# Attention, a routed expert layer and a dense layer on one core: the first job's preparation moved to step ends, masks added per bank, later routing tables made in later jobs

## The chip, the core and the metric

The kernel runs on one core of a Trainium2 chip. The metric is the device time of one execution in microseconds; lower is better. Times inside an execution are counted from the start of its span, the time from the first to the last instruction that the profiler recorded.

The engines are TensorE (PE in the profile, PEld for its weight loads), VectorE (DVE), ScalarE (ACT) and GpSimd (POOL); SyncE (SP) issues most of the transfers. Each engine works through its own instructions in order and waits at a semaphore for what it needs from another one.

## The reference

```python
scores = np.matmul(q, k.transpose(0, 1, 3, 2)) / np.sqrt(64)   # batch 4, 8 heads, 576 positions
rel = pos[:, None] - pos[None, :]
mask_local = (rel >= 0) & (rel < 32)
mask_strided = (rel >= 0) & (pos[None, :] % 32 == pos[:, None] % 32)
scores = where(mask_local if h < 4 else mask_strided, scores, -1e9)
x = softmax(scores) @ v                                        # -> 2304 tokens x 512
logits = x @ w_gate + modality_bias[modality_id]               # 8 experts
e = argmax(logits); gate = softmax(logits)[e]
y[t] = gate[t] * (relu(x[t] @ w1[e]) @ w2[e])                  # 512 -> 1024 -> 512
out = elu(y @ w_in) @ w_out                                    # 512 -> 2048 -> 512
```

All of it is float32. The large products are made of three passes on rounded parts: a value is split into a high part and the rest, which costs ScalarE a copy and VectorE a subtraction.

## The kernel before

**Attention** (line 838 on) takes 32 steps, numbered n from 0: four batches, in each the head pairs 2, 3 (strided mask), 0, 1 (local mask), and two halves of a pair. A step issues, in this order: the scores of step n (`emit_S`, line 983) with their masks and maxima on VectorE and the subtraction of the maxima on GpSimd (line 1010); transposes of q and k for the next pair; transposes of the probabilities of step n-2 (`emit_PT`); the logits of a finished batch, where there is one; transposes of x of step n-5 (`emit_X`); the product with v of step n-3 (`emit_PV`); the exponential of step n-1 on ScalarE; and loads of later steps on SP. A strided unit has eight 72x72 score tiles, four in each of two PSUM banks. One VectorE instruction per tile adds the mask and takes the maximum, and a short readout behind each brings the maximum out (line 1009).

**Routing.** A token goes to the expert of its largest logit. Five jobs of 512 rows are fixed in the program, and a loop at the end takes any that are left (none for these inputs). Job 0 is chosen early, from the first nine blocks of 128 tokens, which exist after step 21: `Router.early` (line 275) ranks the tokens, picks the fullest expert (`star`), makes onehot matrices and a product A on GpSimd (lines 373 and 388), and nine matmuls give the table of row numbers and gates (`finish`, line 390). The rows are gathered by indirect DMAs that GpSimd issues (line 448), scaled by the gates (line 452), transposed by TensorE and split (`trans`, line 459). Weights come by `fetch_to` (SP, two transfers of 256 KB each) and are split by `split_to` (ScalarE and VectorE). This early work is a generator, `early` (line 592). `bg()` runs it on to its next yield; the calls stand in `emit_X` and `emit_PV`, seven or eight in a step. A yield of STEP holds it until `bg.step()`, which each step calls once, behind its product with v.

**Jobs.** A job has eight chunks; a chunk's first product (`gemm1`, lines 485 to 487) and its second (`gemm2`, lines 504 to 506, two chunks later) are cut in four pieces each, a piece being three passes for one of four tiles, and `stream` yields behind each piece. `plan` (line 682) puts other work at piece numbers: the end of attention up to piece 8; logits and choice for the other tokens at 10; ranks of all tokens at 14 (`place`; `rank`, lines 259 and 261, are its matmuls); onehots and A for jobs 1 to 4 at 16 (`first_tables`); the table's matmuls, job 1's number and its gathers at 28; two further tables, for the loop's rows, begun at 30 and 36 and finished at 36 and 44; job 1's scales at 38 and its transposes at 42, 46 and 52; the table of dense places at 53 and 64. The work for jobs 2 to 4 stands inside `stream`. VectorE's copy of a finished table (line 395) and the two or three instructions behind it give the row numbers.

All instructions stand on their engines in the order in which the program issues them.

Of the kernel before, what the change touches and what calls it, by code (L numbers as in the profile page):

```python
# [14 lines left out]
ALU = mybir.AluOpType  # L15
# [14 lines left out]
NT = T // 128  # L30
# [43 lines left out]
class Background:  # L74
# [19 lines left out]

    def step(self):
        self.held = False

    def finish(self):
        while self.gens:
# [69 lines left out]
class Router:  # L169
# [102 lines left out]
        V.tensor_copy(self.lof[:, q, 0:n], self.lo[:, q, 0:n])  # L272
        yield

    def early(self, pool, chosen):

        V = self.tc.nc.vector
        t = lambda shape, dt, name: pool.tile(shape, dt, name=name)
        rank = self.rank(NE, 1)
        yield  # L280
        key = t([128, E], F32, "key")
        kmax = t([128, 1], F32, "kmax")
        z = t([128, NE, E], F32, "z")
        pr = t([128, NE, E], F32, "pr")
        no = t([128, NE], F32, "no")
        sh = [128, NE, E]
        pos = self.pos[:, 0, 0:NE]
        oh = self.oh[:, 0:NE, 1:C]
        V.scalar_tensor_tensor(key, rank[:, NE], 16.0, self.rev, ALU.mult, ALU.add)
        yield  # L290
        V.reduce_max(kmax, key, axis=AX.X)
        yield
        V.tensor_scalar(key, key, kmax, None, ALU.is_equal)
        yield
        V.tensor_tensor(z, oh, key.unsqueeze(1).to_broadcast(sh), ALU.mult)
        yield

        V.scalar_tensor_tensor(pr, rank[:, 0:NE], -4096.0, z, ALU.add, ALU.mult)
        yield
        V.reduce_sum(pos, pr, axis=AX.X)  # L300
        V.tensor_tensor(key[0:1], key[0:1], self.rev[0:1], ALU.mult)
        yield
        V.tensor_scalar(pos, pos, 4096.0, None, ALU.add)
        V.reduce_max(kmax[0:1], key[0:1], axis=AX.X)
        yield
        V.tensor_scalar(self.star, kmax[0:1], -1.0, float(E), ALU.mult, ALU.add)
        chosen()
        yield from self.split_places(0, NE)
        onehot = self.new_onehot(pool)
        yield from self.onehot(0, NE, onehot, self.tc.nc.gpsimd)  # L310
        finish = self.table(pool, onehot, 0, NE, 0, 4, 5, self.idx, self.gates, self.tc.nc.gpsimd)
        yield Background.STEP
        V.tensor_scalar(no, pos, 512.0, None, ALU.is_ge)
        V.tensor_scalar(self.oh[:, 0:NE, 0], pos, 512.0, None, ALU.is_lt)
        yield
        V.tensor_tensor(oh, oh, no.unsqueeze(2).to_broadcast(sh), ALU.mult)
        yield
        finish()
        yield

    def place(self, pool):

# [81 lines left out]
def ffn(tc, ctx, x_dram, part_dram, ident, router, conv, bank, w1, w2, out, run_attention):  # L404
# [46 lines left out]
    def scale(job, c, eng=nc.vector):  # L451
        eng.tensor_scalar(job.xg[c], job.xg[c], job.gate[:, c:c + 1], None, ALU.mult)
# [66 lines left out]
    def new_job(s):  # L519
        word = router.tab[0:1, s, 0:1] if s else router.star  # L520
        e = nc.sync.value_load(word, min_val=0, max_val=E - 1)
        jobs.append(Job(e, None, idx[:, 4 * s:4 * s + 4], gate[:, 4 * s:4 * s + 4]))
# [33 lines left out]
    def fetch_to(g):  # L556
        while loaded[0] <= g:
            s, f = divmod(loaded[0], NCH)
            if s < NS:
                if s == len(jobs):  # L560
                    new_job(s)
                raws[loaded[0]] = fetch(jobs[s], f)
            else:
                fetch2(loaded[0] - NG)
            loaded[0] += 1

    def split_to(g):
        while splits[0] <= g:
            if splits[0] < NG:
                split_w(splits[0] % NW, raws.pop(splits[0]))  # L570
            else:
                split2(splits[0] - NG)
            splits[0] += 1
# [18 lines left out]
    def early():  # L592
        STEP = Background.STEP
        yield from router.choose(0, NE)
        yield from router.early(r_p, lambda: fetch_to(2))
        for c in range(4):
            gather(jobs[0], c)
            yield STEP if c % 2 else None
        for i in range(SPLIT):
            split_to(i)  # L600
            fetch_to(i + AHEAD - SPLIT)
            yield STEP
        for c in range(4):
            scale(jobs[0], c)
            yield STEP if c == 3 else None
        for kk in range(4):
            trans(jobs[0], kk)
            yield STEP if kk % 2 else None

    bg.early = early  # L610
    at = run_attention(bg)
# [4 lines left out]
    def close_b():  # L616
        at.close_b()
        wp = ctx.enter_context(tc.tile_pool(name="w3", bufs=1))
        add_weights(wp, NW - len(WH))
        XT.extend(x_pairs(wp, 2))  # L620
        conv.start(ctx)

    def first_tables():
        oh[0] = router.new_onehot(r_p)
        run(router.onehot(0, NT, oh[0]))
        fin.append(router.table(r_p, oh[0], 0, NT, 4, 20, 5, idx, gate))
        router.blocks(r_p)

    def more_tables(c0):
        fin.append(router.table(r_p, oh[0], 0, NT, c0, c0 + 16, 5, idx, gate))  # L630

    def dense():
        oh[0] = router.new_onehot(r_p)
        run(router.onehot(1, NT, oh[0]))
        fin.append(router.table(r_p, oh[0], 1, NT, 0, NT, 2, idxd, None))

    def open_y():
        rctx.close()
# [2 lines left out]
    def run(gen):  # L641
        for _ in gen:
            pass

    oh, fin = {}, []
    table = lambda: fin.pop()()

    def stream():
# [35 lines left out]
        (3, lambda: at.PV(30)), (3, lambda: at.X(29)), (3, lambda: at.PT(31)),  # L684
        (4, lambda: at.PV(31)), (4, lambda: at.X(30)),
        (5, lambda: at.L(3, 0)), (5, lambda: at.X(31)), (8, lambda: at.L(3, 1)),
        (10, lambda: at.lg(NE, NT)), (10, lambda: run(router.choose(NE, NT))), (10, close_b),
        (14, lambda: run(router.place(r_p))), (16, first_tables),
        (28, table), (28, lambda: new_job(1)), (30, lambda: more_tables(20)), (36, table), (36, lambda: more_tables(36)), (44, table),
        (53, dense), (64, table), (66, open_y),  # L690
    ]
    plan += [(28, lambda c=c: gather(jobs[1], c)) for c in range(4)]
    plan += [(38, lambda c=c: scale(jobs[1], c)) for c in range(4)]
    plan += [(n, lambda kk=kk: trans(jobs[1], kk)) for kk, n in enumerate((42, 46, 52, 52))]
# [18 lines left out]

    lctx = ExitStack()
    x_loop, h_loop = bank("T", "x_ps"), bank("S", "h_ps")
    ahead = [bank("ST"[j], "h2_ps") for j in range(2)]
# [119 lines left out]
def attention(tc, bg, q, k, v, mod, mbias, wg, x_dram, ident, router, bank):  # L838
# [148 lines left out]
    def emit_S(n):  # L987
        b, pr, s = steps[n]
        pi = n // 2
        m, w, nj = shape(pr)  # L990
        pss = [bank("S", f"ps_sc{r}", m, nj, w) for r in range(2)]
        for j in range(nj):
            for r in range(2):

                ro = slice(D * r, D * r + D)
                if pr >= 2:
                    c = (4 * (j % 2) + 2 * s + j // 2) * M
                    ck = c + 32
                else:
                    c = ck = (nj * s + j) * m  # L1000
                nc.tensor.matmul(pss[r][:, j], lhsT=qt[pi % 2][ro, c:c + m],
                                 rhs=kt[pi % 2][ro, ck:ck + w], start=True, stop=True)
        sm = s_p.tile([m, 2 * nj, w], F32, tag="sm", name="sm")
        mx = m_p.tile([m, 2 * nj], F32, tag="mx", name="mx")
        for r in range(2):
            for j in range(nj):
                mk = mask_s if pr >= 2 else (mask_0 if s == 0 and j == 0 else mask_l)
                i = nj * r + j
                nc.vector.tensor_tensor_reduce(sm[:, i], pss[r][:, j], mk, 1.0, -3.0e38, ALU.add, ALU.max, mx[:, i:i + 1])
        nc.gpsimd.tensor_tensor(sm, sm, mx.unsqueeze(2).to_broadcast([m, 2 * nj, w]), ALU.subtract)  # L1010
        st[n] = sm

# [110 lines left out]
    for n in range(NU):  # L1123
        emit_S(n)
        if n + 2 < NU:
            emit_T(n // 2 + 1, 2 * (n % 2))
        if n >= LP:
            emit_PT(n - LP)
        if n + 2 < NU:
            emit_T(n // 2 + 1, 2 * (n % 2) + 1)  # L1130
        if n > LX:
            b, pr, s = steps[n - LX - 1]
            if pr == 1:
                emit_L(b, s)
        if n >= LX:
            emit_X(n - LX)
        if n >= LV:
            emit_PV(n - LV)
        if n == 16 + LX:
            emit_lg(0, NE)  # L1140
            bg.add(bg.early())
        bg.step()
        if n:
            emit_exp(n - 1)
        if n == 5:
            emit_bias()
        if n % 2 == 1:
            p = n // 2 + 3
            if p < 4 * B:
                load_pair(p // 4, PAIRS[p % 4])  # L1150
        if n % 8 == 7 and n + 8 < NU:
            load_vs(n // 8 + 1)
        if n > 8 and n % 8 == 3:
            load_vl(n // 8)
    emit_exp(NU - 1)
    return SimpleNamespace(PT=emit_PT, PV=emit_PV, X=emit_X, L=emit_L, lg=emit_lg, close_a=actx.close, close_b=bctx.close)

# [27 lines left out]
```

## Time and profile before

| | |
|---|---|
| median of 3 runs | 794.57 us (793.63 to 795.36) |
| profiled execution, device time | 794.71 us |
| its span | 793.0 us |
| TensorE busy, share of the span | 763.6 us, 96% |
| VectorE busy | 508.3 us, 64% |
| ScalarE busy | 395.6 us, 50% |
| GpSimd busy | 108.5 us, 14% |
| mean granted clock of TensorE | 0.991 |

Busy time is the union of an engine's instructions. A matmul's end is modelled, so a busy TensorE need not be at its peak. The granted clock is a share of full speed; 0.5 is the lower of two levels. Attention lasts up to about 144 us, the jobs up to about 387 us, the dense layer from there on.

### The profile page before, as it was taken

How to read it: one execution, taken by the hardware profiler on the slowest of the kernel's cores; microseconds unless marked ns; L12 is line 12 of the kernel's file. 1: busy time of each engine (PE TensorE's matmuls, PEld its weight loads, DVE VectorE, ACT ScalarE, POOL GpSimd, SP SyncE). 2: the span in 40 equal slices, each digit the busy share in tenths (PEclk: the TensorE clock that was granted, in tenths of full speed). 3: DMA queues.
4: the chain of work that ended last, by engine and by line, in shares of the span. 5: the costliest groups of instructions: out<-in, count | busy, mean ns of one | idle time of the engine just before them, and what ended most of it. 6: DMA issues, size and time to landing. Idle time of an engine off the chain costs nothing.

```text
span 793.0 us, 12672 instructions
## 1 busy us (share of the span) xinstructions
PE 763.6 (96%) x4513; PEld 636.5 (80%) x4513; DVE 508.3 (64%) x1321; ACT 395.6 (50%) x759; POOL 108.5 (14%) x140
## 2 busy tenths in 40 slices
PE   6999988989999999999899999999999999999995
PEld 5989876868888888888788788888888888888885
DVE  3768779798867677576477565565666454544443
ACT  3667646433544454445376555554565444444442
POOL 4533372022001020000000101001001010101011
PEclk9999999999999999999999999999999999999999
DMA  9587695545566575454232221033133030201111
GB/s 159 120 186 172 151 241 102 153 148 186 179 204 222 172 227 183 163 184 136 93 122 80 94 79 54 27 107 119 41 95 131 1 107 0 84 24 41 66 41 67
DMA packets 100302, 94.37 MB, mean 119 GB/s; under 512 B 45433, under 2 KB 78731, under 8 KB 100235
## 3 DMA queue, kind: packets, MB, share of 16 engines
q1 hardware_dynamic: 95056, 78.79, 34.8%
q0 software_dynamic: 4480, 14.68, 5.4%
q8 instruction: 37, 0.61, 0.3%
q14 instruction: 30, 0.25, 0.1%
q10 hardware_dynamic: 699, 0.04, 0.1%
HBM read 70.95 MB, written 22.54 MB: 118 GB/s over the span
## 4 chain that ended last, share of the span: by engine, by line
PE 50%; POOLq 0%; POOL 0%; DVE 0%; issue 0%
PE o_ps L797 8%; PE o_ps L799 8%; PE o_ps L798 8%; PE h_ps L711 8%; PE h_ps L710 8%; PE h_ps L712 8%; POOLq L1181 0%; POOL out_dram L813 0%; DVE part L812 0%
## 5 line engine op out<-in xcount | busy, mean ns | idle before, releaser
L773 DVE SCALAR_TENSOR_TENSOR t<-e,t 128x512 f32<-128x512 f32 (+1 forms) x80 | 51.1, 638 | 110.7 <-ACT e L771 110.7
L710 PE MATMUL h_ps<-xh,wh 128*128 128x512 f32 (+1 forms) x320 | 119.1, 372 | 2.2 <-PEq L723 2.2
L712 PE MATMUL h_ps<-xh,wl 128*128 128x512 f32 (+1 forms) x320 | 119.3, 373 | 0.0
L711 PE MATMUL h_ps<-xl,wh 128*128 128x512 f32 (+1 forms) x320 | 119.2, 372 | 0.0
L797 PE MATMUL o_ps<-wh,gh 128*128 128x512 f32 x288 | 113.3, 393 | 0.0
L798 PE MATMUL o_ps<-wl,gh 128*128 128x512 f32 x288 | 112.9, 392 | 0.0
L799 PE MATMUL o_ps<-wh,gl 128*128 128x512 f32 x288 | 112.9, 392 | 0.0
L770 ACT ACTIVATE t<-h_ps 128x512 f32<-128x512 f32 (+1 forms) x80 | 44.2, 552 | 99.8 <-PE h_ps L712 92.3
L775 ACT CAST gh<-r 128x512 fp32r<-128x512 f32 (+1 forms) x80 | 46.2, 578 | 81.5 <-DVE r L774 81.5
L776 DVE TENSOR_TENSOR gl<-r,gh 128x512 fp32r<-128x512 f32 (+1 forms) x80 | 51.1, 639 | 51.5 <-ACT gh L775 51.5
L469 DVE TENSOR_TENSOR wl<-wraw,wh 128x1024 fp32r<-128x1024 f32 x56 | 69.2, 1235 | 12.8 <-ACT wh L468 11.0
L710 PEld LDWEIGHTS h_ps<-xh,wh 128*128 128x128 f32 x320 | 60.6, 189 | 14.3 <-issue 2.6
L711 PEld LDWEIGHTS h_ps<-xl,wh 128*128 128x128 f32 x320 | 60.6, 189 | 11.9
L712 PEld LDWEIGHTS h_ps<-xh,wl 128*128 128x128 f32 x320 | 60.5, 189 | 11.0
L504 PE MATMUL y_ps<-hh,wh 128*128 128x512 f32 x160 | 64.6, 404 | 0.0
L797 PEld LDWEIGHTS o_ps<-wh,gh 128*128 128x128 f32 x288 | 54.1, 188 | 12.5 <-DVE o L808 0.7
L799 PEld LDWEIGHTS o_ps<-wh,gl 128*128 128x128 f32 x288 | 54.1, 188 | 12.1
L485 PE MATMUL h_ps<-xh,wh 128*128 128x512 f32 x160 | 63.7, 398 | 0.0
L506 PE MATMUL y_ps<-hh,wl 128*128 128x512 f32 x160 | 63.3, 395 | 0.0
L505 PE MATMUL y_ps<-hl,wh 128*128 128x512 f32 x160 | 63.2, 395 | 0.0
L798 PEld LDWEIGHTS o_ps<-wl,gh 128*128 128x128 f32 x288 | 54.1, 188 | 11.1
L487 PE MATMUL h_ps<-xh,wl 128*128 128x512 f32 x160 | 62.9, 393 | 0.0
(180 smaller groups left out, 1393.4 us busy)
## 6 DMA issues: line engine op xcount, KB each, us to landing
wraw<-in_moe_w_dram SPq DMA_DIRECT2D x80, 256.0 KB
raw<-in_moe_w_in_dram SPq DMA_DIRECT2D x16, 512.0 KB
raw<-in_moe_w_out_dram SPq DMA_DIRECT2D x16, 512.0 KB
w_f<-cv_r SPq DMA_DIRECT2D x32, 256.0 KB
wraw<-w_f SPq DMA_DIRECT2D x16, 512.0 KB
part_dram<-o POOLq DMA_DIRECT2D x18, 256.0 KB, 3.0
part<-part_dram SPq DMA_DIRECT2D x18, 256.0 KB
qn<-in_q_dram SPq DMA_DIRECT2D x8, 288.0 KB
```

What stands on the lines that cost most here:

```text
L469: nc.vector.tensor_tensor(WL[i], raw, WH[i].bitcast(F32), ALU.subtract)
L485: nc.tensor.matmul(ps, lhsT=a, rhs=job.xh[kk], start=kk == 0, stop=False)
L487: nc.tensor.matmul(ps, lhsT=b, rhs=job.xh[kk], start=False, stop=kk == 3)
L504: nc.tensor.matmul(ps, lhsT=a, rhs=hh, start=f == 0, stop=False)
L505: nc.tensor.matmul(ps, lhsT=a, rhs=hl, start=False, stop=False)
L506: nc.tensor.matmul(ps, lhsT=b, rhs=hh, start=False, stop=f == NCH - 1)
L710: nc.tensor.matmul(ps[:, 0:n], lhsT=a, rhs=yh, start=kk == 0, stop=False)
L711: nc.tensor.matmul(ps[:, 0:n], lhsT=a, rhs=yl, start=False, stop=False)
L712: nc.tensor.matmul(ps[:, 0:n], lhsT=b, rhs=yh, start=False, stop=kk == 3)
L797: nc.tensor.matmul(ps, lhsT=a, rhs=WH[i][:, 512:1024], start=first, stop=False)
L798: nc.tensor.matmul(ps, lhsT=a, rhs=WL[i][:, 512:1024], start=False, stop=False)
L799: nc.tensor.matmul(ps, lhsT=b, rhs=WH[i][:, 512:1024], start=False, stop=last)
```

## The change

Six things are done.

1. `flush` empties the background work up to its next STEP, at the end of each attention step. The STEPs in `Router.early` and `early` stand at other places, and the fetches of job 0's weights are begun one by one, not three together.
2. Job 0's scales are made by GpSimd, not by VectorE.
3. For strided units VectorE adds the mask to a whole bank (72x288) in one instruction, twice, and takes all eight maxima with one reduction over 72x576.
4. The three instructions that mark the tokens which job 0 took leave the early work and stand behind the choice for the other tokens, at piece 10 (`others`).
5. The two further tables are begun at pieces 84 and 104 and finished at 100 and 116.
6. The dense places are made three blocks at a time, every fourth piece from 120 on, and finished at 164. Onehots and products have a pool of their own, `late`, closed before the loop.

```diff
 class Background:
+    def flush(self):
+        while self.gens and not self.held:
+            self()
...
-    def early(self, pool, chosen):
+    def early(self, pool, chosen, more):
...
         V.scalar_tensor_tensor(pr, rank[:, 0:NE], -4096.0, z, ALU.add, ALU.mult)
-        yield
+        yield Background.STEP
...
         chosen()
         yield from self.split_places(0, NE)
+        yield Background.STEP
         onehot = self.new_onehot(pool)
-        yield from self.onehot(0, NE, onehot, self.tc.nc.gpsimd)
+        for i, _ in enumerate(self.onehot(0, NE, onehot, self.tc.nc.gpsimd)):
+            yield Background.STEP if i == 1 else None
         finish = self.table(pool, onehot, 0, NE, 0, 4, 5, self.idx, self.gates, self.tc.nc.gpsimd)
+        more()
         yield Background.STEP
-        V.tensor_scalar(no, pos, 512.0, None, ALU.is_ge)
-        V.tensor_scalar(self.oh[:, 0:NE, 0], pos, 512.0, None, ALU.is_lt)
-        yield
-        V.tensor_tensor(oh, oh, no.unsqueeze(2).to_broadcast(sh), ALU.mult)
-        yield
         finish()
         yield
+
+        def others():
+            V.tensor_scalar(no, pos, 512.0, None, ALU.is_ge)
+            V.tensor_scalar(self.oh[:, 0:NE, 0], pos, 512.0, None, ALU.is_lt)
+            V.tensor_tensor(oh, oh, no.unsqueeze(2).to_broadcast(sh), ALU.mult)
+
+        self.others = others
...
     def early():
         STEP = Background.STEP
         yield from router.choose(0, NE)
-        yield from router.early(r_p, lambda: fetch_to(2))
+        yield STEP
+        yield from router.early(r_p, lambda: fetch_to(0), lambda: fetch_to(1))
         for c in range(4):
             gather(jobs[0], c)
-            yield STEP if c % 2 else None
-        for i in range(SPLIT):
-            split_to(i)
-            fetch_to(i + AHEAD - SPLIT)
-            yield STEP
+            yield STEP if c == 1 else None
+        split_to(0)
+        fetch_to(2)
+        yield STEP
+        split_to(1)
+        fetch_to(3)
+        yield
         for c in range(4):
-            scale(jobs[0], c)
-            yield STEP if c == 3 else None
+            scale(jobs[0], c, nc.gpsimd)
+            yield STEP if c == 1 else None
         for kk in range(4):
             trans(jobs[0], kk)
-            yield STEP if kk % 2 else None
+            yield STEP if kk % 2 == 0 else None
...
-    def dense():
-        oh[0] = router.new_onehot(r_p)
-        run(router.onehot(1, NT, oh[0]))
-        fin.append(router.table(r_p, oh[0], 1, NT, 0, NT, 2, idxd, None))
+    def dense(i):
+        if i == 0:
+            oh[0] = router.new_onehot(late[0])
+            oh[1] = router.onehot(1, NT, oh[0])
+        next(oh[1], None)
+        if i == NT // 3:
+            fin.append(router.table(late[0], oh[0], 1, NT, 0, NT, 2, idxd, None))
...
-        (10, lambda: at.lg(NE, NT)), (10, lambda: run(router.choose(NE, NT))), (10, close_b),
+        (10, lambda: at.lg(NE, NT)), (10, lambda: run(router.choose(NE, NT))), (10, lambda: router.others()), (10, close_b),
         (14, lambda: run(router.place(r_p))), (16, first_tables),
-        (28, table), (28, lambda: new_job(1)), (30, lambda: more_tables(20)), (36, table), (36, lambda: more_tables(36)), (44, table),
-        (53, dense), (64, table), (66, open_y),
+        (28, table), (28, lambda: new_job(1)), (66, open_y),
+        (84, lambda: more_tables(20)), (100, table), (104, lambda: more_tables(36)), (116, table), (164, table),
     ]
+    plan += [(120 + 4 * i, lambda i=i: dense(i)) for i in range(NT // 3 + 1)]
...
         for r in range(2):
+            if pr >= 2:
+                nc.vector.tensor_tensor(sm[:, nj * r:nj * r + nj], pss[r], mask_s.unsqueeze(1).to_broadcast([m, nj, w]), ALU.add)
+                continue
             for j in range(nj):
-                mk = mask_s if pr >= 2 else (mask_0 if s == 0 and j == 0 else mask_l)
+                mk = mask_0 if s == 0 and j == 0 else mask_l
                 i = nj * r + j
                 nc.vector.tensor_tensor_reduce(sm[:, i], pss[r][:, j], mk, 1.0, -3.0e38, ALU.add, ALU.max, mx[:, i:i + 1])
+        if pr >= 2:
+            nc.vector.reduce_max(mx, sm, axis=AX.X)
         nc.gpsimd.tensor_tensor(sm, sm, mx.unsqueeze(2).to_broadcast([m, 2 * nj, w]), ALU.subtract)
...
         if n > 8 and n % 8 == 3:
             load_vl(n // 8)
+        bg.flush()
```

## Rows read from the trace of the kernel before

**Rows 1.** The page's first part: busy us (share of the span) and instructions.

```profile
PE 763.6 (96%) x4513; PEld 636.5 (80%) x4513; DVE 508.3 (64%) x1321; ACT 395.6 (50%) x759; POOL 108.5 (14%) x140
```

**Rows 2.** Busy time by stretch; behind the engines granted clock, DMA share, GB/s.

```profile
60.00:80.00 20.00, 20.00 (x294) 18.86 (x291) 17.70 (x125) 14.36 (x38) 7.52 (x6) 1.00 0.73 174
...
92.00:94.00 2.00, 1.08 (x13) 0.94 (x14) 1.97 (x13) 1.45 (x4) 0.10 (x1) 1.00 0.00 0
108.00:114.00 6.00, 5.58 (x68) 5.41 (x69) 5.00 (x29) 3.20 (x7) 4.83 (x5) 0.72 1.01 286
...
124.00:136.00 12.00, 8.61 (x82) 6.66 (x79) 11.75 (x46) 6.57 (x13) 3.79 (x3) 1.00 0.27 66
...
174.00:180.00 6.00, 5.65 (x33) 4.74 (x34) 5.24 (x11) 0.00 (x0) 3.01 (x3) 0.72 0.98 335
```

**Rows 3.** TensorE in order of time, attention: scores of steps 24, 29, 30, table, q.

```profile
95.78 0.74 PE L1001 MATMUL ps_sc<-kt,qt 64*72 64x72 f32 x16
...
108.42 0.37 PE L393 MATMUL tab_ps<-A,onehot 128*128 128x20 bf16 x9 [1.91 <-POOL A L388]
...
115.65 0.44 PE L976 MATMUL ps_tr<-ident,qn 96*128 96x96 f32 x3 [1.32 <-DMA qn<-in_q_dram]
...
119.10 0.90 PE L1001 MATMUL ps_sc<-kt,qt 64*96 64x128 f32 x12
...
123.41 0.90 PE L1001 MATMUL ps_sc<-kt,qt 64*96 64x128 f32 x12
```

**Rows 4.** ScalarE in order of time: the exponential of the logits.

```profile
92.22 0.26 ACT L239 ACTIVATE lg_ex<-lg_d 128x72 f32<-128x72 f32 x1 [1.20 <-DVE lg_d L234]
```

**Rows 5.** VectorE in order of time: step 24's first masked maximum, last readout; marking product.

```profile
98.08 0.21 DVE L1009 CUSTOM_DVE_ANT_0 sm<-ps_sc,mask_s 72x72 f32<-72x72 f32 x1
...
99.30 0.07 DVE L1009 DVE_READ_ACCUMULATOR2_ANT mx<- 72x1 f32 x1
...
106.87 2.71 DVE L316 TENSOR_TENSOR oh<-oh,no 128x72 bf16<-128x72 bf16 x1
```

**Rows 6.** Groups of VectorE by line, 60 to 260 us: count, busy us, mean ns.

```profile
L1066 DVE TENSOR_TENSOR xs<-ps_v,rs 72x256 f32<-72x256 f32 x20 | 7.6, 415 | 0.3
...
L340 DVE TENSOR_REDUCE pos<-places 128x36 f32<-128x324 f32 x1 | 0.5, 491 | 0.0
```

**Rows 7.** GpSimd in order of time: subtractions, onehots, A, gathers of job 1.

```profile
99.54 1.15 POOL L1010 TENSOR_TENSOR sm<-sm,mx 72x576 f32<-72x576 f32 x1 [2.62 <-ACT sm L1014]
101.55 5.26 POOL L373 TENSOR_SCALAR onehot<-iota,pos_lof 128x128 bf16<-128x128 bf16 x9 [0.86 <-DVE rs L1061]
...
107.87 0.50 POOL L388 TENSOR_TENSOR A<-oa,vals 128x180 bf16<-128x180 bf16 x1
...
123.40 1.47 POOL L1010 TENSOR_TENSOR sm<-sm,mx 96x768 f32<-96x768 f32 x1 [5.64 <-DVE mx L1009]
...
171.52 1.57 POOL L448 DMA_INDIRECT xg<-x_dram,idx  x1 [14.89 <-DMA wraw<-in_moe_w_dram]
...
176.67 0.95 POOL L448 DMA_INDIRECT xg<-x_dram,idx  x1 [0.30 <-issue]
```

**Rows 8.** TensorE in order of time, first job: ranks, two tables, job 1's transposes.

```profile
154.19 0.25 PE L259 MATMUL rank<-oh,triu 128*128 128x171 bf16 x1
...
164.98 0.82 PE L393 MATMUL tab_ps<-A,onehot 128*128 128x80 bf16 x18
...
174.35 1.16 PE L393 MATMUL tab_ps<-A,onehot 128*128 128x80 bf16 x18 [2.90 <-DVE A L388]
...
180.81 0.72 PE L463 MATMUL x_ps<-ident,xg 128*128 128x128 f32 x4
```

**Rows 9.** VectorE in order of time, first job: the first table's copy, job 1's scales.

```profile
170.34 0.23 DVE L395 COPY tab_sb<-tab_ps 128x80 f32<-128x80 f32 x1
...
179.42 1.72 DVE L452 TENSOR_SCALAR xg<-xg,gates 128x512 f32<-128x512 f32 x4
```

**Rows 10.** The tile xg, 80 to 270 us: the 16 gathers, from issue to landing.

```profile
DMA to landing us min/median/max: 4.0/5.2/7.6
```

More of the change, by code (lines that the diff above doesn't have):

```diff
@@ L621, in close_b @@
         conv.start(ctx)
+        late.append(tctx.enter_context(tc.tile_pool(name="late", bufs=1)))
     def first_tables():
-        oh[0] = router.new_onehot(r_p)
+        oh[0] = router.new_onehot(late[0])
         run(router.onehot(0, NT, oh[0]))
-        fin.append(router.table(r_p, oh[0], 0, NT, 4, 20, 5, idx, gate))
+        fin.append(router.table(late[0], oh[0], 0, NT, 4, 20, 5, idx, gate))
         router.blocks(r_p)
     def more_tables(c0):
-        fin.append(router.table(r_p, oh[0], 0, NT, c0, c0 + 16, 5, idx, gate))
-    def dense():
-        oh[0] = router.new_onehot(r_p)
-        run(router.onehot(1, NT, oh[0]))
-        fin.append(router.table(r_p, oh[0], 1, NT, 0, NT, 2, idxd, None))
+        fin.append(router.table(late[0], oh[0], 0, NT, c0, c0 + 16, 5, idx, gate))
+    def dense(i):
+        if i == 0:
+            oh[0] = router.new_onehot(late[0])
+            oh[1] = router.onehot(1, NT, oh[0])
+        next(oh[1], None)
+        if i == NT // 3:
+            fin.append(router.table(late[0], oh[0], 1, NT, 0, NT, 2, idxd, None))
     def open_y():
@@ L643, in run @@
             pass
-    oh, fin = {}, []
+    oh, fin, late = {}, [], []
+    tctx = ExitStack()
     table = lambda: fin.pop()()
@@ L712, in up_mm @@
             nc.tensor.matmul(ps[:, 0:n], lhsT=b, rhs=yh, start=False, stop=kk == 3)
+    tctx.close()
     lctx = ExitStack()
```

## The prediction

> **What bounds the kernel now.** The page's first part comes first: TensorE is busy for 763.6 of 793.0 us [rows 1], so at most about 29 us are idle, and only idle time and slow clock are there to be won. The busy time by stretch says where: from 60 to 80 us TensorE is full with VectorE at 17.70 of 20 us; in 92 to 94 it lacks 0.92 us, in 124 to 136 it lacks 12.00 - 8.61 = 3.39 us with VectorE at 11.75 [rows 2]. Then TensorE's own timeline: it waits 1.91 us for GpSimd's product A before the first job's table, 1.32 us for a load of q [rows 3], and 2.90 us for VectorE's A before the second table [rows 8]. The granted clock is at 0.72 in the 6 us after each of the two longest of these waits [rows 2]: the engine, just idle, drops to the lower of its two levels (1.2 instead of 2.4 GHz) for a while, at a loss of 0.28 x 6 = 1.7 us each. The stretch 124 to 136, with shorter waits among its matmuls, stays at 1.00. So the change bears on some 1.9 + 1.3 + 0.9 + 3.4 + 2.9 + 2 x 1.7 = 13.8 us, the most it could win.
>
> **How the pieces move.** The routing work waits in chunks that end at a STEP. The hold is lifted after a step's transposes and value products, and the new flush then empties one chunk at the end of each step. So chunks go out whole, behind each engine's work of that step: the choice of experts after step 21, ranks after 22, places and the first weight fetch after 23, six onehots after 24, three onehots with A after 25, the table with two gathers after 26, two gathers and the first split after 27, the second split and scales 0 and 1 after 28, scales 2 and 3 and the first transposes after 29, the rest after 30 and 31.
>
> **Masks.** Eight masked maxima start at 98.08 and the last readout ends at 99.37: 1.29 us of VectorE [rows 5]. Two additions of 72x288 cost about 0.415 x 288/256 = 0.47 each, a maximum over 576 columns 0.491 x 576/324 = 0.87, from the nearest rows [rows 6], so 1.8 us; with overlap such as the eight show, 1.5. That is 0.2 to 0.5 us more for each of 16 units, not less. I take nothing on the path: TensorE is full there while VectorE has a tenth free [rows 2]. Without this cover, in steps 24 to 27, four units would give 0.8 to 2 us; the bank freed after one addition gives some of it back.
>
> VectorE's groups add up to far more, since each of the eight takes 0.21 and a readout 0.07, 2.3 us a unit; but they start 0.15 apart. The Trainium skill (VectorE: DVE Perf Modes, Rules for kernel authors) says to minimise the number of instructions, because chaining them saves nothing. By that rule the edit would free 0.8 us a unit; by the row it frees none. That is the third rival below.
>
> **Choice of experts.** ScalarE's exponential of the logits waits 1.20 us for VectorE, and the scores' exponential is queued behind it [rows 4]; that is the 0.92 us in 92 to 94. It now stands one step earlier, behind the exponential that was late. Take -0.9 (bounds 0 and -0.9).
>
> **Weights of the first job.** Three fetches of 2 x 256 KB left together ahead of the last pair's q and k. Now one leaves after step 23, behind the loads of that step; the second is queued behind the last pair. SP's load of the expert number still waits for VectorE, with only the next store of x behind it. The wait for q goes: -1.3 (0 to -1.3).
>
> **First table.** On GpSimd the subtraction of step 24 starts 99.54 - 95.78 = 3.8 us after that step's scores; 1.15 + 5.26 + 1.15 + 0.50 = 8.1 us must pass before A exists, cut in two or not [rows 3, 7]. So A comes 11.9 us after the scores. TensorE needs three steps, 108.42 - 1.91 - 95.78 = 10.7 us, or 10.1 if small waits go [rows 3]. It waits 1.2 to 1.8: I take 1.7 in place of 1.91, -0.2 (bounds -0.8, +0.5), and the slow stretch behind it stays.
>
> **Scales on GpSimd, transposes one step sooner.** No row shows this scale. GpSimd's onehots take 5.26/9 = 0.58 us for 128 columns; the subtractions 1.15 for 576 and 1.47 for 768 give 1.67 ns a column, 1.05 us at 512 [rows 7]. Lower bound 0.6 (as a onehot, whatever the width), upper 2.3 (four onehots); I take 1.2, the subtraction's line plus what a onehot lies above it. Scales 2 and 3 are queued behind the subtraction of step 29, which began at 123.40, 4.3 us after that step's scores at 119.10 [rows 3, 7]. So they end at 4.3 + 1.47 + 2.4 = 8.2 us. TensorE is through with step 29 after 123.41 - 119.10 = 4.3 us and stands before a transpose that needs all four rows: 3.9 us; with VectorE 1 us earlier, 2.9. I take 3.4 (2.2 at 0.6 us a scale, 5.6 at 2.3). This is a new wait, and everything of steps 30 and 31 is behind it on TensorE; a third slow stretch, +1.7, follows as behind the wait of 1.91. In return it lets the other engines catch up: of the 3.39 us, 0.4 are left, -3.0 (0 to -3.4).
>
> Attention: -0.9 - 1.3 - 0.2 + 3.4 + 1.7 - 3.0 = -0.3 us.
>
> **During the first job.** The three VectorE instructions taken out of the early routing run before the ranks of all tokens, which TensorE now reaches at 154.19 without a wait [rows 8]: about 0.2 us each, +0.7 (0.3 if part is hidden; up to 2.7 when GpSimd is busy, as the product did at 106.87 [rows 5]).
>
> The wait of 2.90 before the second table goes, and a wait stands where that time leads to. The transposes of job 1 keep their places, 14 pieces after the first table, which starts at 164.98; eight pieces lie between that table and the present wait, (174.35 - 2.90 - 164.98 - 0.8)/8 = 0.7 us each [rows 8]. So TensorE gets there 0.8 + 14 x 0.7 = 10.6 us after that start. But their rows depend on VectorE's copy of the first table, 170.34, 5.4 us after it [rows 9], and the order on VectorE up to there is unchanged; the first gather starts at 171.52, 6.5 us after, the fourth at 176.67, 11.7 after (10.3 if the first two are as short as the others) [rows 7]; landing takes 4.0 to 7.6 us [rows 10], the scale 0.43 [rows 9]. So the last rows are ready 14.7 to 16.1 us after the table at the fastest landing, and the transpose ends at about 15.6, against 180.81 + 0.72 - 164.98 = 16.55 now [rows 8]: -0.9 (-1.6 to +1.0). The wait is nearly 5 us, and the clock falls behind it instead of before: +1.7 (0 if it doesn't). The second table's 18 matmuls (1.16 us at the low clock [rows 8]) now follow where TensorE is full instead of ahead of those transposes: +0.6. Sum: 0.7 - 0.9 + 1.7 + 0.6 = +2.1 us (bounds -0.7 and +4.5).
>
> The later tables and the dense places are the same instructions, spread over jobs 1 to 4; their products are made 12 or more pieces before TensorE asks for them. Nothing.
>
> **Sum.** The profiled execution took 794.71 us (span 793.0, 1.7 around it), 0.14 above the median of 794.57. 794.7 - 0.3 + 2.1 = 796.5 us.
>
> **Rivals.**
>
> 1. *Faster: GpSimd is quick.* A scale of 0.6 us makes the wait 2.2; if that wait and a first table's wait of 1.3 leave the clock alone, attention gives -0.9 - 1.3 - 0.6 + 2.2 - 3.0 - 1.7 = -5.3, with the job's +2.1: 791.5 us. For it: a one-input operation, and 124 to 136 kept its clock [rows 2]. Against: onehots, also one-input, lie above the subtractions' line. It decides below 0.8 us a scale. The Trainium skill (GPSIMD Engine Reference, Engine selection) keeps elementwise work on VectorE but calls one-input operations roughly line rate; by its clock of 1.2 GHz 512 columns would be some 0.4 us, an estimate, plus a start. No row here shows 512 columns.
> 2. *Slower: GpSimd sets the pace.* At 2.3 us a scale the wait is 5.6, and scales 0 and 1 hold the subtraction of step 29 by another 0.5: +2.7, 799.2 us. For it: 0.58 us for only 128 columns [rows 7].
> 3. *The masks relieve VectorE.* With 0.8 us less a unit, the subtraction of step 24 starts 0.8 earlier, the first table's wait is 0.9, and its slow stretch goes: -2.5, 794.0 us. Against: the eight overlap [rows 5].
>
> That the change does what it says for the later tables is not in doubt; that this saves TensorE's time is: the wait is moved from a table to the gathered rows.
>
> **How the numbers follow.** 0.2% (1.6 us) is about what a measurement of this kernel can tell from no change. The forecast has 0.47, its own range 794.5 to 798.5: 0.02 faster, 0.20 within, 0.25 slower. Rival 1 has 0.25: 0.23 faster, 0.02 within. Rival 2 has 0.16, all slower. Rival 3 has 0.12: 0.03, 0.08, 0.01. Together 0.28 faster, 0.30 within, 0.42 slower. The range reaches to the other cases: 791.0 to 800.0 us.
>
> **What would show it.** Right: a TensorE wait for GpSimd of 1.2 to 2.4 us before the first table, one of 2 to 6 us before the first job's first transpose, released by a scale; no wait for q; one of 4 to 6 us before job 1's first transposes, released by VectorE's scale, with a clock below 1 behind it; no wait at a later table; strided units of 1.5 us or more on VectorE. Wrong: scales much below 0.8 us, a full TensorE at the end of step 29, gathers of job 1 issued before VectorE's copy time, or fewer slow stretches than two.

## The result and the profile after

Six executions of each on one chip: 799.73 us median with the change (798.34 to 806.46), 794.87 before (793.63 to 798.60). The ratio is 1.0075 with a 95% interval from 1.0046 to 1.0104: slower, and by 4.9 us from median to median where 1.9 were forecast. The profiled execution took 799.71 us (span 798.0, mean granted clock 0.988).

First the busy time of the page, then busy time by stretch: behind the engines stand granted clock, DMA share and GB/s.

```profile
PE 765.8 (96%) x4513; PEld 637.6 (80%) x4513; DVE 507.5 (64%) x1109; ACT 395.9 (50%) x759; POOL 117.6 (15%) x144
```

```profile
60.00:80.00 20.00, 19.97 (x287) 18.78 (x286) 18.56 (x77) 15.21 (x40) 7.53 (x6) 1.00 0.79 182
92.00:94.00 2.00, 2.00 (x25) 1.68 (x23) 1.79 (x10) 1.25 (x4) 1.00 (x1) 1.00 0.00 0
108.00:114.00 6.00, 6.00 (x73) 5.68 (x70) 3.96 (x13) 3.50 (x7) 5.18 (x5) 0.72 1.15 286
120.00:126.00 6.00, 2.20 (x25) 1.71 (x23) 3.02 (x19) 1.60 (x3) 6.00 (x4) 1.00 0.81 208
126.00:136.00 10.00, 9.90 (x83) 9.06 (x84) 6.69 (x34) 5.34 (x11) 1.52 (x3) 0.66 0.12 31
174.00:180.00 6.00, 2.77 (x12) 1.83 (x10) 1.66 (x2) 0.48 (x1) 3.66 (x3) 1.00 0.95 310
180.00:190.00 10.00, 6.83 (x24) 5.12 (x25) 6.40 (x11) 3.29 (x5) 0.00 (x0) 0.66 0.21 77
```

Against [rows 2]: 92 to 94 is full now. From 124 on the many short waits are gone, but 120 to 126 has one hole of 3.8 us, and behind it the clock is at 0.66 for 10 us. The same happens from 174 on: a hole of 3.2 us, more of it after 180, and 0.66 again. TensorE's waits, by what released them (us in total, times, longest), and TensorE in order of time:

```profile
PE x_ps L474 <- DVE xg L463: 6.3, 3, 3.1
...
PE x_ps L474 <- POOL xg L463: 3.9, 2, 2.7
PE tab_ps L404 <- POOL A L399: 2.6, 1, 2.6
PE ps_tr L997 <- DMA qn<-in_q_dram: 1.6, 2, 1.0
...
PE x_ps L474 <- DVE tab_sb L406: 0.4, 1, 0.4
```

```profile
107.81 0.37 PE L404 MATMUL tab_ps<-A,onehot 128*128 128x20 bf16 x9 [2.59 <-POOL A L399]
...
124.56 0.33 PE L474 MATMUL x_ps<-ident,xg 128*128 128x128 f32 x1 [2.68 <-POOL xg L463]
126.10 0.47 PE L474 MATMUL x_ps<-ident,xg 128*128 128x128 f32 x1 [1.21 <-POOL xg L463]
...
155.09 0.23 PE L264 MATMUL rank<-oh,triu 128*128 128x171 bf16 x1 [0.31 <-DVE oh L328]
...
165.86 0.82 PE L404 MATMUL tab_ps<-A,onehot 128*128 128x80 bf16 x18
...
178.59 0.30 PE L474 MATMUL x_ps<-ident,xg 128*128 128x128 f32 x1 [2.12 <-DVE xg L463]
181.97 0.47 PE L474 MATMUL x_ps<-ident,xg 128*128 128x128 f32 x1 [3.09 <-DVE xg L463]
183.54 1.05 PE L474 MATMUL x_ps<-ident,xg 128*128 128x128 f32 x2 [1.09 <-DVE xg L463]
```

One matmul waits, then one or two more, as the rows come one by one. The wait of 2.90 us before the second table [rows 8] is gone; 6.3 us stand at job 1's first transposes in its place. What the rows there waited for is seen on VectorE and on SP's queue:

```profile
171.19 0.23 DVE L406 COPY tab_sb<-tab_ps 128x80 f32<-128x80 f32 x1
...
173.94 1.23 DVE L480 TENSOR_TENSOR wl<-wraw,wh 128x1024 fp32r<-128x1024 f32 x1 [0.25 <-ACT wh L479]
177.96 0.48 DVE L463 TENSOR_SCALAR xg<-xg,gates 128x512 f32<-128x512 f32 x1 [2.79 <-DMA xg<-x_dram,idx]
181.44 0.48 DVE L463 TENSOR_SCALAR xg<-xg,gates 128x512 f32<-128x512 f32 x1 [2.99 <-DMA xg<-x_dram,idx]
183.00 1.07 DVE L463 TENSOR_SCALAR xg<-xg,gates 128x512 f32<-128x512 f32 x2 [1.08 <-DMA xg<-x_dram,idx]
```

```profile
173.10 0.38 SPq L486 DMA_DIRECT2D wraw<-in_moe_w_dram  x1
173.69 0.35 SPq L488 DMA_DIRECT2D wraw<-in_moe_w_dram  x1
...
175.20 0.38 SPq L486 DMA_DIRECT2D wraw<-in_moe_w_dram  x1
175.77 0.35 SPq L488 DMA_DIRECT2D wraw<-in_moe_w_dram  x1
```

In the kernel before, this weight split stood behind two products A, and the fetch that needs its buffer left behind it (VectorE, then SP's queue):

```profile
176.70 1.66 DVE L388 TENSOR_TENSOR A<-oa,vals 128x1440 bf16<-128x1440 bf16 x1
178.28 1.21 DVE L469 TENSOR_TENSOR wl<-wraw,wh 128x1024 fp32r<-128x1024 f32 x1
```

```profile
179.52 0.38 SPq L475 DMA_DIRECT2D wraw<-in_moe_w_dram  x1
```

It left at 179.52, as the scales began [rows 9]. Now the split runs at 173.94 and the fetch leaves at 175.20, among the gathers. Job 1's four gathers took, by the tile's view, before and now:

```profile
DMA to landing us min/median/max: 4.0/4.3/4.6
```

```profile
DMA to landing us min/median/max: 5.1/6.3/7.1
```

GpSimd's scales in order of time, and the new mask unit on VectorE (step 24, two additions and a maximum):

```profile
118.12 3.37 POOL L463 TENSOR_SCALAR xg<-xg,gates 128x512 f32<-128x512 f32 x2
121.50 1.47 POOL L1036 TENSOR_TENSOR sm<-sm,mx 96x768 f32<-96x768 f32 x1
122.94 3.10 POOL L463 TENSOR_SCALAR xg<-xg,gates 128x512 f32<-128x512 f32 x2
```

```profile
97.89 0.81 DVE L1028 TENSOR_TENSOR sm<-ps_sc,mask_s 72x288 f32<-72x288 f32 x2
98.80 0.75 DVE L1035 TENSOR_REDUCE mx<-sm 72x8 f32<-72x576 f32 x1
```

To see where time goes, I cut the profiled executions at three of TensorE's instructions: the first job's table, the table of jobs 1 to 4, and job 2's first transposes. The stretches, in us:

| kernel | to first table | to jobs' table | to job 2's transposes | to the end | span |
|---|---|---|---|---|---|
| before | 108.42 | 56.56 | 59.17 | 568.85 | 793.0 |
| changed | 107.81 | 58.05 | 62.16 | 569.98 | 798.0 |
| changed, again | 107.76 | 56.85 | 62.74 | 569.85 | 797.2 |

Of the 5.0 us between the first two spans, 0.9 arose up to the jobs' table, 3.0 in the first job and 1.1 behind it. In the second profile of the changed kernel it is -0.4, 3.6 and 1.0: what is lost in the first job is common to both, what is lost up to the jobs' table is not.

### The profile page after: what moved, and what is told of

Same layout as the page of the kernel before. It is cut to its first block, busy times and chain, and to the rows that moved or that the text cites. A ratio compares the mean times of both kernels' runs of the same rounds, so it can differ in the third digit from the quotient of the medians.

```text
span 798.0 us, 12467 instructions
## 1 busy us (share of the span) xinstructions
PE 765.8 (96%) x4513; PEld 637.6 (80%) x4513; DVE 507.5 (64%) x1109; ACT 395.9 (50%) x759; POOL 117.6 (15%) x144
## 5 line engine op out<-in xcount | busy, mean ns | idle before, releaser
L497 PE MATMUL h_ps<-xl,wh 128*128 128x512 f32 x160 | 63.2, 395 | 0.0
```

The costliest lines, as they stand in the source:

```text
L497: nc.tensor.matmul(ps, lhsT=a, rhs=job.xl[kk], start=False, stop=False)
```

## The experiments

Theory 1: the loss is made at job 1's first transposes. Theory 2: it is made in attention, at GpSimd's scales and the transposes one step sooner. Theory 3: the masks. Theory 4: the three instructions moved to the ranks. Each ratio below is against the kernel before on the same chip. Its median on these chips runs from 794.55 to 796.12 us, so a difference of a microsecond or so between medians of different experiments says little by itself.

**Base.** The changed kernel again.

> The changed kernel itself again, for a steadier base beside the others of this group: 799 to 801 us.

800.48 us, ratio 1.0047 (1.0017 to 1.0077). With the first six, some 800 us.

**Job 1's transposes later.**

```diff
-    plan += [(38, lambda c=c: scale(jobs[1], c)) for c in range(4)]
-    plan += [... enumerate((42, 46, 52, 52))]
+    plan += [(45, lambda c=c: scale(jobs[1], c)) for c in range(4)]
+    plan += [... enumerate((48, 50, 52, 53))]
```

> The changed kernel with job 1's scales at piece 45 (not 38) and its transposes at 48, 50, 52, 53 (not 42, 46, 52, 52); nothing else. Theory 1 (the loss is made at job 1's first transposes, where TensorE waits 6.3 us for scaled rows and then runs some 3.4 us' worth at the low clock): the wait falls below 1.5 us, the low clock behind it goes, and the time falls by 5 to 9 us against the changed kernel, to 791 to 795 us. Theory 2 (the loss is made in attention by GpSimd's scales and the early transposes): what is gained at piece 42 is only handed to the next wait in the first job; 798 to 800 us. Theory 3 (the new masks cost VectorE's time): as theory 2.

796.25 us, 1.0010 (0.9990 to 1.0031): some 4 us back, where theory 1 expected 5 to 9. The stretch to job 2's transposes falls from 62.16 to 58.04. The wait is 2.6 us, not under 1.5: six pieces later are not late enough for all rows.

**The old places of the later tables**, and, the other way round, **those places alone in the kernel before.**

```diff
-        (84, lambda: more_tables(20)), (100, table), (104, lambda: more_tables(36)), (116, table), (164, table),
+        (30, lambda: more_tables(20)), (36, table), (36, lambda: more_tables(36)), (44, table),
+        (53, lambda: [dense(i) for i in range(NT // 3 + 1)]), (64, table),
...
-    plan += [(120 + 4 * i, lambda i=i: dense(i)) for i in range(NT // 3 + 1)]
```

> The changed kernel with the two further tables begun at pieces 30 and 36 and finished at 36 and 44, and the dense places at 53 and 64, as before. Theory 1: the wait of 2.9 us before the second table is back, the weight fetch that ran beside job 1's gathers leaves some 5 us later again, the gathers land in 4.0 to 4.6 us, and the wait at job 1's first transposes is under 1 us; 2 to 4 us faster than the changed kernel, 796 to 798 us. Theory 2: no better than the changed kernel, 799 to 801 us. Theory 3: as theory 2.

> The kernel before with the new places of the two further tables and of the dense places alone; attention as before. Theory 1 (what is lost in the first job comes from emptying VectorE there, whatever attention does): the wait of 2.9 us before the second table goes, the fetch leaves earlier, a wait of 5 to 7 us appears at job 1's first transposes; 2 to 4 us slower than the kernel before, 797 to 799 us. Rival (it comes from the attention part, which makes the job's later waits fall otherwise): 794 to 796 us.

The first: 796.74 us, 1.0024 (1.0000 to 1.0047); the wait of 2.9 us is back, the one at the transposes is 0.2 us, the gathers land in 4.3 to 4.9 us. The second: 800.98 us, 1.0073 (1.0044 to 1.0103), 6.4 us slower than the kernel before and more than theory 1 expected, with 6.0 us of waits at those transposes. So the plan of the tables alone makes a loss as large as the whole change's.

**The same plan in the kernel before, with the transposes later** (the edit of the second experiment).

> The kernel before with the new places of the further tables and of the dense places (800.98 us alone) and job 1's scales and transposes at pieces 45 and 48 to 53. If the loss lies in the places 38 and 42, which the change left where they were: 3 to 5 us less, 796 to 798 us. If it lies in the tables' new places themselves: 799 to 801 us.

796.12 us, 1.0008 (0.9981 to 1.0035). About 5 of the 6 us were in the pieces 38 and 42, which the change had left alone.

**One fetch held back.**

```diff
-            split_to(min(g + SPLIT, NG + LAG - 2 + SPLIT))
-            fetch_to(min(g + AHEAD, NG + LAG - 2 + SPLIT))
+            if g != 5:
+                split_to(min(g + SPLIT, NG + LAG - 2 + SPLIT))
+                fetch_to(min(g + AHEAD, NG + LAG - 2 + SPLIT))
...
+    plan += [(38, lambda: split_to(5 + SPLIT)), (38, lambda: fetch_to(5 + AHEAD))]
```

> The changed kernel with one weight split (VectorE's and ScalarE's part of it, and the fetch behind it) moved from piece 37 to piece 38, behind job 1's scales: so the fetch that left at 175.2 us beside the gathers cannot leave before the scales. Theory 1a (the gathers land in 5.1 to 7.1 us, not 4.0 to 4.6, because this fetch shares the transfer engines with them): landing 4.0 to 5.0 us, the wait at job 1's first transposes 6.3 falls to 3 to 4.5 us, time 2 to 3.5 us under the changed kernel, 796 to 798 us. Theory 1b (the gathers land late by themselves): landing unchanged at 5 to 7 us and time within 1 us of the changed kernel, 799 to 801 us.

798.24 us, 1.0043 (1.0024 to 1.0062): by the medians 1.5 to 2.2 us less than the changed kernel, between the two theories, but the intervals of the ratios overlap (the base has 1.0017 to 1.0077), so the gain in time is not clear of noise. The trace shows more. VectorE in order of time:

```profile
176.80 0.49 DVE L463 TENSOR_SCALAR xg<-xg,gates 128x512 f32<-128x512 f32 x1 [4.46 <-DMA xg<-x_dram,idx]
179.23 0.48 DVE L463 TENSOR_SCALAR xg<-xg,gates 128x512 f32<-128x512 f32 x1 [1.94 <-DMA xg<-x_dram,idx]
179.89 0.49 DVE L463 TENSOR_SCALAR xg<-xg,gates 128x512 f32<-128x512 f32 x1 [0.18 <-DMA xg<-x_dram,idx]
180.54 0.49 DVE L463 TENSOR_SCALAR xg<-xg,gates 128x512 f32<-128x512 f32 x1 [0.16 <-DMA xg<-x_dram,idx]
180.94 1.22 DVE L480 TENSOR_TENSOR wl<-wraw,wh 128x1024 fp32r<-128x1024 f32 x1
```

The last row is ready at 181.03, 16.6 us after the table's start at 164.46. In the changed kernel it is 184.07 - 165.86 = 18.2, before 181.14 - 164.98 = 16.2. So with the split and the fetch held back the rows are ready 1.6 us sooner. Other profiles agree: with this fetch behind the gathers' issue the rows are ready after 16.2, 16.5, 16.6 and 17.0 us (before, old tables, here, and the old tables with job 0's transposes later, further down), with it among the gathers after 17.8 to 18.5 in the seven that scale at piece 38. Of the kernels that scale at piece 45 (further down) it is 17.5 to 18.2 in five with it among the gathers, 16.5 and 17.3 in two with it held. But the landings are still 5.1 to 6.3 us, so the fetch is not all that slows them; what else does stayed open. And the edit did one thing more: GpSimd's second gather was issued in less time, so that the third and the fourth left 0.7 us sooner (changed kernel, then here):

```profile
174.29 1.70 POOL L459 DMA_INDIRECT xg<-x_dram,idx  x1 [0.30 <-issue]
```

```profile
172.94 0.95 POOL L459 DMA_INDIRECT xg<-x_dram,idx  x1 [0.30 <-issue]
```

Split and fetch were moved together, so no run tells how much of the 1.6 us belongs to the fetch on the transfer engines and how much to this.

**Job 0's scales on VectorE; its transposes one step later; the old masks.**

```diff
-            scale(jobs[0], c, nc.gpsimd)
+            scale(jobs[0], c)
```

> The changed kernel with job 0's four scales on VectorE again, at their new place. Theory 1: the wait of 3.9 us before the first job's first transposes falls to 0.5 to 2 us; its two slow stretches go or stay with it; attention gives back 1 to 3 us, and the job-1 wait of 6.3 us is unchanged: 797 to 799 us. Theory 2: this is the whole loss: 795 us or less. Theory 3: no change, 799 to 800 us.

```diff
             scale(jobs[0], c, nc.gpsimd)
-            yield STEP if c == 1 else None
+            yield STEP if c % 2 else None
         for kk in range(4):
             trans(jobs[0], kk)
-            yield STEP if kk % 2 == 0 else None
+            yield STEP if kk % 2 else None
```

> The changed kernel with job 0's transposes one step later, as before the change (two in step 30, two in step 31), and the scales still on GpSimd. If in attention the price is the place of the first transpose (theory 2a), the wait of 3.9 us and the low clock behind it go: 2 to 4 us under the changed kernel, 796 to 798 us. If it is GpSimd's scales themselves (theory 2b: they delay the subtractions of steps 29 and 30, whoever waits), the wait comes back at the exponentials of those steps: 799 to 801 us.

```diff
-            if pr >= 2:
-                nc.vector.tensor_tensor(sm[...], pss[r], mask_s..., ALU.add)
-                continue
...
+                mk = mask_s if pr >= 2 else (mask_0 if s == 0 and j == 0 else mask_l)
-        if pr >= 2:
-            nc.vector.reduce_max(mx, sm, axis=AX.X)
```

> The changed kernel with the eight masked maxima of a strided unit as before, one instruction a tile. Theory 3 (each strided unit costs VectorE 0.3 to 0.4 us more, and in steps 24 to 27 that delays what TensorE waits for): 1 to 3 us faster, with the wait before the first job's table of 2.6 us down by 0.5 or more. Theories 1 and 2: within 0.5 us of the changed kernel.

Scales on VectorE: 797.15 us, 1.0024 (1.0001 to 1.0047); the wait falls from 3.9 to 2.05 us. Transposes later, scales still on GpSimd: 794.60 us, 0.9996 (0.9979 to 1.0014), 5 to 6 us back, though job 1's wait of 6.5 us is untouched. This is more than was expected. Busy time by stretch, columns as above:

```profile
120.00:126.00 6.00, 5.21 (x67) 4.67 (x66) 5.42 (x32) 3.55 (x8) 5.99 (x5) 1.00 0.47 140
126.00:132.00 6.00, 6.00 (x62) 5.34 (x61) 5.29 (x21) 5.21 (x10) 2.46 (x2) 1.00 0.37 101
132.00:138.00 6.00, 6.00 (x61) 5.65 (x60) 3.79 (x11) 2.88 (x9) 0.00 (x0) 1.00 0.15 37
```

The hole has shrunk to 0.8 us, the clock stays at 1.00, and the short waits of the kernel before don't come back: TensorE is full from 126 on. Old masks: 800.01 us, 1.0062 (1.0035 to 1.0088), no gain, though the wait before the first table falls from 2.59 to 1.95 us. Theory 3 falls.

**The marking instructions in attention, behind job 0's last transposes.**

```diff
         for kk in range(4):
             trans(jobs[0], kk)
...
+        router.others()
...
```

The call at piece 10 is taken out.

> The changed kernel with the three instructions that mark job 0's tokens behind job 0's last transposes in attention, not behind the choice for the other tokens. Theory 4 (they delay TensorE's ranks): the wait of 0.3 us there goes and the time falls by 0.3 to 1 us, to 799 to 800 us. Otherwise no difference from 800.5 us.

799.12 us, 1.0045 (1.0024 to 1.0066). The wait of 0.3 us at the ranks is gone. It is 1.4 us under the base, but the executions overlap (796.5 to 800.9 against 798.7 to 802.0): a small share at most.

**Both repairs together, and more.** Scales on VectorE with job 1 later; transposes one step later with job 1 later; the same with the fetch held to piece 42; the table and all behind it one step later, scales on VectorE, job 1 later; transposes one step later with the old tables; and the third of these with the scales on VectorE.

> Both repairs in one: job 1's scales and transposes later, job 0's scales on VectorE. If the two losses are separate (each was worth 2.6 to 3.5 us alone), they add: 5.5 to 7 us under the changed kernel, 793 to 795 us, level with the kernel before or up to 2 us under it. If they are one (a loss only handed on), no better than either alone: 796 to 797 us.

> The changed kernel with job 0's transposes one step later (scales still on GpSimd) and job 1's scales and transposes at pieces 45 and 48 to 53. If the two losses are separate (5.1 and 3.5 us alone): 790 to 793 us, 2 to 5 us under the kernel before. If job 1's wait only takes up what attention gave: 794 to 796 us.

> The same as the run before it, with one weight split and so one fetch held back from piece 37 to 42, out of the gathers' way. Theory 1a: holding the fetch brought job 1's last rows from 18.2 to 16.5 us after the table's start; here TensorE's remaining wait for these rows falls by 1 to 2 us: 0.5 to 2 us under that run. Rival: the wait is covered already, or the held split is late for its own chunk: no better or up to 2 us worse.

> The changed kernel with job 1's scales and transposes late as in those runs, and the whole chain of job 0 from its table on one step later: table after step 27, gathers after 27 and 28, scales on VectorE and the transposes after 30 and 31. If the wait of 2.6 us before the first table and the low clock behind it are a loss of their own: they go, and the time is 788 to 791 us. If the chain is then late at its end (gathers collide with the loads of the last pair, the job's first product waits): 793 us or more.

> The attention part alone, with job 0's transposes at their place of before: the changed kernel with the old places of the further tables (796.74 us) and job 0's transposes one step later. If the two parts' losses add (3.7 us for the tables' places, 5.9 us for the transposes): 790 to 792.5 us, under the kernel before by 2 to 5 us. If not: 794 us or more.

> The best run so far (787.78 us) with job 0's scales on VectorE. If GpSimd's scales still cost something where nothing waits long for them (a wait of 0.8 us at the second group of transposes): 0.5 to 1.5 us less, 786 to 787.5 us. If GpSimd has the room: 787 to 789 us.

| kernel | median us | ratio (95%) | to jobs' table | to job 2's transposes |
|---|---|---|---|---|
| scales on VectorE, job 1 later | 793.06 | 0.9975 (0.9953 to 0.9998) | 53.74 | 56.18 |
| transposes and job 1 later | 790.83 | 0.9930 (0.9900 to 0.9961) | 54.57 | 57.90 |
| and the fetch held | 787.78 | 0.9896 (0.9867 to 0.9926) | 52.86 | 55.50 |
| table one step later | 791.99 | 0.9951 (0.9930 to 0.9973) | 56.01 | 56.08 |
| transposes later, old tables | 789.90 | 0.9931 (0.9904 to 0.9958) | 52.61 | 60.06 |
| all, scales on VectorE | 785.70 | 0.9874 (0.9843 to 0.9906) | 51.65 | 54.71 |

The losses add, so they are two. The held fetch came out 3.1 us under the run before it, more than the 0.5 to 2 expected; but of the 4.3 us between the two profiles 1.7 lie in the stretch up to the jobs' table, which the edit does not touch, so not all of it is the edit's. With the table one step later (its two stretches therefore start at another place in the work) the wait before it is gone, but a load of q is waited for again (1.2 us) and the first transpose for a scale (3.2 us): the chain is only shifted into its own end. The last row is 1.3% under the kernel before, with the change's masks, flush and later tables kept. In it TensorE waits for job 1's rows once, for 0.6 us, and the wait of 2.5 us before the first table is still there. Around job 0's and job 1's transposes the stretches are full but for 0.8 us in the last:

```profile
114.00:120.00 6.00, 6.00 (x77) 5.43 (x76) 5.71 (x32) 4.79 (x11) 1.96 (x2) 1.00 1.23 220
120.00:126.00 6.00, 6.00 (x72) 5.36 (x73) 5.86 (x29) 3.95 (x10) 2.93 (x2) 1.00 0.45 136
...
170.00:180.00 10.00, 9.22 (x46) 7.00 (x45) 6.25 (x11) 4.62 (x8) 0.51 (x1) 1.00 0.69 230
```

## Why the prediction was right and wrong

The direction and the places were right, though "slower" had a chance of only 0.42; the size was not. Step by step:

- **Masks.** Forecast 1.5 to 1.8 us a unit, measured 99.55 - 97.89 = 1.66 [rows 5]. "Nothing on the path" is right for the whole; the first table pays 0.64 us for them. The Trainium skill's rule (VectorE: DVE Perf Modes, Rules for kernel authors) would have made three instructions cheaper than eight with their readouts; here they take 0.37 us more, since the eight overlapped. The third rival is out.
- **Choice of experts, weights.** As forecast: 92 to 94 is full, and the wait of 1.32 us for q [rows 3] is gone.
- **First table.** 2.59 us, outside its bounds (1.1 to 2.4); the low clock behind it as forecast.
- **Scales and transposes.** The wait of 3.4 us came out as 2.68 + 1.21 = 3.9, with a scale of 1.55 us instead of 1.2. Rival 1 needed 0.8. By the Trainium skill (GPSIMD Engine Reference, Engine selection) a one-input operation runs at roughly line rate; the rows of this case do not agree for a scale of 512 columns: 1.55 us on GpSimd, 0.48 on VectorE. The slow stretch cost 0.34 x 10 = 3.4 us, twice the forecast; in the second profile of the same kernel it cost 1.7:

```profile
126.00:136.00 10.00, 9.96 (x94) 9.03 (x95) 7.66 (x37) 6.27 (x12) 2.74 (x2) 0.83 0.18 47
```

One argument here was false: that the wait "lets the other engines catch up" and so pays for the short stalls after 124. With the transposes a step later there is a wait of 0.8 us and no stall. The 3.0 us I set against the wait were to be had without it. That attention's sum still came out near the forecast is luck: the slow stretch and the first table were dearer than forecast, and what made up for them is not settled (below).
- **Marking instructions.** 0.7 forecast, a wait of 0.3 seen at the ranks.
- **During the first job: the step that failed.** The prediction had job 1's first transposes end 15.6 us after the table's start, 0.9 sooner than before. They end at 183.54 + 1.05, 18.7 us after it: 2.2 later than before, so this one term is 3.1 us off, and the wait there is 6.3 us, not "nearly 5". The gathers were issued as forecast (6.5 and 11.7 us after the table's start), but they landed in 5.1 to 7.1 us where I took the fastest, 4.0, of a range that reached 7.6 [rows 10]. About half of the 3.1 us goes with something I did not look for: what the freed VectorE does next. It splits a weight block 4.3 us sooner, SP's next fetch leaves among the gathers, and with both held back the rows are ready 1.6 us sooner. The rest stayed open: without that fetch the landings still took 5.1 to 6.3 us. Busy time by stretch behind these waits, columns as above:

```profile
180.00:182.00 2.00, 0.03 (x1) 0.03 (x1) 0.48 (x1) 0.00 (x0) 0.00 (x0) 0.68 0.97 359
182.00:184.00 2.00, 0.91 (x2) 0.34 (x2) 0.91 (x3) 0.00 (x0) 0.00 (x0) 0.50 0.08 27
184.00:186.00 2.00, 1.89 (x6) 1.59 (x6) 1.93 (x5) 0.52 (x1) 0.00 (x0) 0.50 0.00 0
186.00:188.00 2.00, 2.00 (x7) 1.53 (x7) 1.32 (x3) 1.46 (x4) 0.00 (x0) 0.61 0.00 0
```

At the low clock up to 184.6 us TensorE mostly waits anyway; behind it, 1.4 us at 0.50 and 2 at 0.61 lose 1.5 us, near the 1.7 forecast. With the 0.6 of the second table and 0.3 at the ranks: 2.2 + 1.5 + 0.6 + 0.3 = 4.6 us, against 0.3 + 3.0 + 1.1 = 4.4 in the stretches above; forecast were 2.1. (Not in this sum: a wait of 0.4 us at a later table, next item, and 0.8 us less waiting where the dense layer starts.) The other 0.9 us of the miss is attention's: -0.3 forecast, 0.9 - 0.3 = +0.6 measured up to the jobs' table; in the second profile it is -0.7, and the whole miss is the first job's. The forecast's upper bound for the first job, +4.5, does not follow from its terms, whose upper ends add up to 2.7 + 1.0 + 1.7 + 0.6 = 6.0.
- **Later tables.** "Nothing" was forecast, and TensorE does not wait for their products. But behind the second of them transposes of job 2 wait 0.4 us for VectorE's copy of the table (the last line of the waits above), in every profile with the new places. This wait, that table (0.66 us up to the next product) and the one of the dense places (0.46) stand behind job 2's first transposes now, 1.5 us, and cover the 1.1 us there.
- **Rivals.** Rival 2's time, 799.2, is near the result, but its mechanism (2.3 us a scale, a wait of 5.6) is not what happened.

Not settled: the idle time and the clock of 100 to 140 us would make attention some 2 us longer than the stretches above show; and the plan alone cost 6 us where taking it out of the changed kernel gave 3 to 4.

## What to carry to other kernels

When an early wait is removed, the consumers planned behind it at fixed places reach their data sooner than the data comes: move them in the same edit, or the wait only changes its name. Follow the engine that was freed to the next thing it does: here it released a buffer, and with it a fetch that left among the gathers.

## What the runs showed of the hardware

The same wait did not cost the same clock each time: behind the attention wait two profiles of one kernel lost 3.4 and 1.7 us. Spans of one kernel differ along with the clock: two executions of the kernel before had 791.7 us at a mean granted clock of 0.991 and 797.6 at 0.982. Job 1's four indirect gathers of 128 rows landed in 4.0 to 4.6 us before and in 5.1 to 7.1 us with the change; with one weight fetch kept from beside them it was 5.1 to 6.3, so that fetch accounts for a part. Issuing one took GpSimd 0.95 to 1.72 us in the kernel before. GpSimd's scale of 128x512 took 1.55 us (two in 3.10), and two took up to 3.86 in the kernel of the held fetch; what slowed these is not shown.
